# One core, attention and two MLP layers: another order of VectorE and ScalarE work at four seams, and 384 + 384 column blocks

## The chip, the core and the metric

The kernel runs on one core of a Trainium2 chip. The metric is the time of one execution on the device in microseconds (us), median of the runs shown; lower is better. Five engines work side by side, each through its own queue in order: TensorE (PE in the rows; PEld is its weight load), VectorE (DVE), ScalarE (ACT), GpSimd (POOL) and SyncE (SP, which here only issues DMAs). PE writes its results to PSUM, eight banks of 512 fp32 columns; DVE and ACT read them there. A semaphore wait at the head of a queue holds everything behind it.

## What is computed

Attention in clusters, then two MLP layers, all in fp32. The tokens of both batches are one axis of 1536.

```python
# attention: B=2, H=8, S=768, D=64; a query sees the keys of its own cluster
scores = where(q_cluster == k_cluster, q @ k.T / sqrt(D), -1e9)
attn = softmax(scores) @ v
x = attn.transpose(0, 2, 1, 3).reshape(B * S, H * D)          # 1536 x 512
# first layer: d_ff 2048
h = x @ w_in
x = (maximum(h, 0) + log1p(exp(-abs(h)))) @ w_out             # 1536 x 512
# second layer: d_ff 1536
g = x @ w_gate
out = (g / (1 + exp(-g)) * (x @ w_val)) @ w_out2
```

Weights come as fp64 and are narrowed on the chip. Each fp32 product is made of three matmuls on rounded halves: high by high, high by low, low by high.

## The kernel before

**Attention.** 16 heads go in pairs, in 96 steps of one 128-row tile each. `step(i)` issues for several tiles at once: the scores of tile i (`sc`, matmul L509, DVE row maximum L517), the exponential of tile i-1 (`ex`, ACT L525), the transposes of tile i-2 (`tr`, L541; ACT copies the high half `th` L547, DVE subtracts for the low half `tl` L548) and a third of the product with V (`pv`, L558). After the last pair `rec` makes the reciprocals `r` of the row sums on DVE, `rec_rows` transposes them on PE (L603), copies them (`R<-mps`, L606) and sends them through DRAM and back; `fin` multiplies with them and writes `XH` and `XL`, the halves of the first layer's input.

**Weights.** `w_narrow` and `w_split` take a block in three tasks: `first` (ACT absolute value, L123), `second` (two DVE passes, L125 and L128) and `third` (two DVE passes L132 and L135, then the high half `whi` L149 and the low half `wlo` L150, and the next load is issued on SP). There are three buffers for raw blocks, `raw`, and two for `m`. Tasks wait in the list `todo`; `pump` and `pump2` take some of them at set places in the code, and that alone sets the order in which they stand on DVE and ACT.

**First layer.** `h_unit(f)` makes one of 16 tiles of 128 hidden columns: 36 matmuls of 512 columns (L818) into three banks, then ACT and DVE empty the banks (`e`, `r`), two ACT passes (exponential, logarithm), a DVE sum (L888), and the halves `gh` (ACT, L858) and `gl` (DVE, L859). `y_group(g)` multiplies two such tiles with their rows of `w_out`: four groups of 18 matmuls (L908), each into three banks, which DVE adds to `acc` (L922). Units and groups alternate: two units, one group, eight times. The eight banks go round in the order in which they are asked for, so a tile's third bank can be one that an earlier tile's reader still holds. In the last group ACT also casts `acc` to `YH` (L924), and the differences `YL` go to DVE (five) or POOL (seven; L930).

**Second layer.** Of its 12 tiles, two (`plain_unit`) are plain: gate and val products of 36 matmuls each (L818), ACT Silu on the gate (L1072), a DVE product (L1081), halves (`a_half`, L973 and L974). The other ten (`s_unit`) use products of quarters; these need sums of the quarters of `acc` (`t_sums`, L1032 to L1035, four DVE subtractions of 1536 columns), and their halves `Th` (ACT, L1041) and `Tl` (DVE, L1045). Each of the ten makes seven products (`prod`, L1124): 12 matmuls that alternate 512 and 256 columns. The copy of the first (L1156) must empty its banks before the third. `o_piece` (L1096) multiplies with `w_out2` between them.

Of the kernel before, what the change touches and what calls it, by code (L numbers as in the profile page):

```python
# [11 lines left out]
F32 = mybir.dt.float32  # L12
# [28 lines left out]
def kernel(  # L41
# [18 lines left out]
    nc = tc.nc  # L60
# [130 lines left out]
    for f in range(NF2):  # L191
        stream += (pair_of(f + 1) if NPLAIN <= f + 1 < NF2 else []) + last_of(NF1 + f)
    W = {}
    loaded_t = {}
    n_load = [0]
# [9 lines left out]
    def split_tasks(batch):  # L205
# [25 lines left out]
            begun.add(tasks[-1])  # L231
        return tasks


    todo = collections.deque()

# [549 lines left out]
    for i in range(N_IT + 1):  # L786
# [8 lines left out]
        if i == 26:  # L795
            pump(2)
    rec(NP - 1)
    rec_rows(NP - 1)
    sctx.close()

# [60 lines left out]


    acc = mp.tile([128, KD, NTOK], F32, tag="acc", name="acc")
    g_t = {}

    def h_unit(f, banks=None):
        if banks is None:
            banks = [bank() for _ in range(NCH)]
            w = need(W, ("in", f))
            for half in range(2):  # L870
                proj(XH, XL, w, banks, range(2 * half, 2 * half + 2))
                pump()
# [20 lines left out]
        return [log_part, sum_part, split_part], split_tasks(batches.pop(0))  # L893

    def y_group(g):
        last = g == NF1 // 2 - 1
# [2 lines left out]
        for d0 in range(0, KD, nd):  # L899
# [15 lines left out]
            for n, bk in enumerate(banks):  # L915
# [15 lines left out]
            if not last:  # L931
                pump()

    soft0, split0 = h_unit(0, h0)
    soft1, split1 = h_unit(1, h1)
    todo.extend(split0 + [soft0[0], soft1[0], soft0[1], soft1[1], soft0[2], soft1[2]] + split1)
    pump(8)
    for g in range(NF1 // 2):
        if 2 * g + 2 < NF1:
            for f in (2 * g + 2, 2 * g + 3):  # L940
                soft, split = h_unit(f)
                if f < NF1 - 2:
                    todo.extend([soft[0]] + split[:3] + [soft[1]] + split[3:6] + [soft[2]] + split[6:])
                else:
                    first_do(soft + split[:3])
                    todo.extend(split[3:])
# [6 lines left out]
    HT = NTOK // 2  # L953
    CH = (slice(0, 512), slice(512, HT))
    outv = out.rearrange("(b p t) d -> b p t d", b=B, t=NT)
    a_t = {}
    high_on.append(1)

    def pieces_of(f):

        if f == NF2 - 1:
# [16 lines left out]
        for _ in range(-(-len(todo) // steps)):  # L978
            todo.popleft()()

    S_t, T_t = {}, {}

    def pair_tasks(f):

# [43 lines left out]

    def t_sums():

        q = [[acc[:, 2 * k:2 * k + 2, HT * t:HT * t + HT] for t in range(2)] for k in range(2)]
        nc.vector.tensor_tensor(out=q[0][0], in0=q[0][1], in1=q[0][0], op=ALU.subtract)  # L1032
        nc.vector.tensor_tensor(out=q[0][1], in0=q[1][1], in1=q[0][1], op=ALU.subtract)
        nc.vector.tensor_tensor(out=q[1][1], in0=q[1][1], in1=q[0][0], op=ALU.subtract)
        nc.vector.tensor_tensor(out=q[1][0], in0=q[1][0], in1=q[1][1], op=ALU.subtract)  # L1035
# [11 lines left out]
        tasks = []  # L1047
        for n, x in ((3, q[0][1]), (2, q[1][1]), (4, q[1][0]), (1, q[0][0])):
            tasks += [functools.partial(high, n, x), functools.partial(low, n, x)]
        return tasks  # L1050

    def plain_unit(f):
        gb = [bank() for _ in range(NCH)]
        wg = need(W, ("gate", f))
        if f == 0:
            vb = [bank() for _ in range(NCH)]
            wv = need(W, ("val", f))
            proj(YH, YL, wg, gb, range(KD - 1))
            pump2(4)
            proj(YH, YL, wv, vb, range(KD - 1))  # L1060
            pump2(3)
            proj(YH, YL, wg, gb, range(KD - 1, KD))
            proj(YH, YL, wv, vb, range(KD - 1, KD))
            pump2(2)
        else:
            for half in range(2):
                proj(YH, YL, wg, gb, range(2 * half, 2 * half + 2))
                pump2(4 - half)
        sg = tp.tile([128, NTOK], F32, tag="e", name="sg")
        for c in range(NCH):  # L1070
            cs = slice(512 * c, 512 * c + 512)
            nc.scalar.activation(out=sg[:, cs], in_=gb[c], func=AF.Silu)  # L1072
        if f:
            vb = [bank() for _ in range(NCH)]
            wv = need(W, ("val", f))
            for half in range(2):
                proj(YH, YL, wv, vb, range(2 * half, 2 * half + 2))
                pump2(2 - half)
        for c in range(NCH):
            cs = slice(512 * c, 512 * c + 512)  # L1080
            nc.vector.tensor_tensor(out=sg[:, cs], in0=vb[c], in1=sg[:, cs], op=ALU.mult)  # L1081

        def home():
            a_t[f] = pieces_of(f)

        return [home] + [functools.partial(a_half, f, sg, n) for n in range(2)]

    def o_piece(g, n, tag="O"):
        bk = psx.tile([128, 2, 512], F32, tag=tag, name="ob")
        for ff in range(2):  # L1090
            hi, lo = need(W, ("out2", 2 * g + ff))
            ah, al = (x[n // 3] for x in a_t[2 * g + ff])
            for t in range(2):
# [21 lines left out]
    def s_unit(f):  # L1115
# [3 lines left out]
        def prod(dst, group, at, x, first=False):  # L1119
            hi, lo = group  # L1120
            for kk in range(2):
                for wt, part in ((hi, 0), (hi, 1), (lo, 0)):
                    for cs in CH:
                        nc.tensor.matmul(  # L1124
                            dst[:, cs],
                            lhsT=wt[:, at + kk, :],
                            rhs=x(part, kk)[:, cs],
                            start=(first and kk == 0 and wt is hi and part == 0),
                            stop=(kk == 1 and wt is lo),
                            skip_group_check=True,  # L1130
# [17 lines left out]
            pump2(left[0])  # L1148
            left[0] -= 1

        t1, t2 = slice(0, HT), slice(HT, NTOK)
        sg = tp.tile([128, NTOK], F32, tag="e", name="sg")
        x = psx.tile([128, 1024], F32, tag="X", name="x")[:, 0:HT]
        prod(x, g1, 0, quarter(0, 0), True)
        p1 = p1_p.tile([128, HT], F32, tag="p1", name="p1")
        nc.scalar.copy(p1, x)  # L1156
        more()
        w = psx.tile([128, 1024], F32, tag="W", name="w")[:, 0:HT]
        prod(w, g2, 0, tq(3), True)
        nc.scalar.copy(sg[:, t2], w)  # L1160
        more()
# [13 lines left out]
        y = psx.tile([128, 1024], F32, tag="Y", name="y")[:, 0:HT]  # L1175
# [11 lines left out]
        a_half(f, sg, 0)  # L1187
        a_half(f, sg, 1)

    side = [tp.tile([128, NTOK], F32, tag="s", name="side") for _ in range(2)]  # L1190
    todo.extend(t_sums())
    todo.extend(split_tasks(last_of(NF1)))
    todo.extend(plain_unit(0))
    todo.extend(pair_tasks(2))
    todo.extend(split_tasks(last_of(NF1 + 1)))
    rest = plain_unit(1)
    while todo:
        todo.popleft()()
# [63 lines left out]
```

## Time and profile before

| | us |
|---|---|
| median of 3 runs | 815.05 |
| runs | 814.87 to 816.88 |
| profiled execution | 813.9 |
| its span, first to last instruction | 812.1 |
| PE busy in the span | 791.0 |
| DVE busy | 654.5 |
| ACT busy | 500.8 |
| POOL busy | 163.0 |

The profiled execution is 1.15 us under the median; 1.8 us of it lie outside the span. The mean granted PE clock is 0.994 of full speed. A matmul's record is longer than its step, since matmuls overlap in the pipeline; so the pace of PE is read from the starts of neighbours.

### The profile page before, as it was taken

What the parts mean: (1) busy time and instruction counts of PE and PEld (TensorE: products, weight loads), DVE (VectorE), ACT (ScalarE), POOL (GpSimd) and SP (SyncE); (2) the same over time, 40 slices, a digit from 0 to 9 for tenths busy, and PEclk for the clock granted to TensorE, in tenths of its full rate; (3) what the DMA queues carried; (4) which work ended last, traced back from release to release, by engine and by line L of the source; (5) the groups of instructions that cost most, each with busy time, mean ns of one, the idle gap of its engine ahead of it and who ended that gap; (6) DMA issues with size and microseconds to landing.
All of it is one profiled execution on the core that took longest, in us unless ns stands there. A gap on an engine that the chain in (4) does not pass through costs nothing.

```text
span 812.1 us, 12093 instructions
## 1 busy us (share of the span) xinstructions
PE 791.0 (97%) x4485; PEld 689.6 (85%) x4485; DVE 654.5 (81%) x1047; ACT 500.8 (62%) x893; POOL 163.0 (20%) x160
## 2 busy tenths in 40 slices
PE   8999999999999999999999999989999999999997
PEld 7898999999998778888888887867888888888886
DVE  6988988888895997989879778889777777777763
ACT  5888889889895587365563744355544655555520
POOL 5736456555522000000000000400000101011100
PEclk9999999999999999999999999999999999999999
DMA  7875865675411322222121210012435676767454
GB/s 177 238 180 128 204 145 145 168 164 138 98 40 31 104 78 78 76 81 78 52 78 55 76 52 28 25 39 92 155 132 115 144 147 138 154 120 142 85 176 155
DMA packets 69339, 91.57 MB, mean 113 GB/s; under 512 B 29376, under 2 KB 52000, under 8 KB 69280
## 3 DMA queue, kind: packets, MB, share of 16 engines
q1 hardware_dynamic: 64688, 79.40, 34.6%
q0 software_dynamic: 3024, 11.01, 9.0%
q8 instruction: 35, 0.57, 0.3%
q10 hardware_dynamic: 1568, 0.39, 0.2%
q14 instruction: 24, 0.20, 0.1%
HBM read 51.41 MB, written 17.35 MB: 85 GB/s over the span
## 4 chain that ended last, share of the span: by engine, by line
PE 81%; DVE 12%; ACT 3%; DMA 2%; issue 1%; POOL 0%; DVEq 0%; ACTq 0%; SPq 0%; POOLq 0%
PE bank L908 14%; PE bank L818 13%; PE ob L1096 12%; PE x L1124 10%; PE ops L558 7%; PE tps L541 7%; PE sps L509 7%; PE w L1124 5%; PE y L1124 3%; PE mps L383 1%; PE sims L420 1%; DVE m L135 1%; DVE m L132 1%; DVE acc L922 1%; DVE wlo L150 1%
## 5 line engine op out<-in xcount | busy, mean ns | idle before, releaser
L548 DVE TENSOR_TENSOR tl<-tps,th 128x384 fp32r<-128x384 f32 x192 | 98.8, 550 | 14.8 <-ACT th L547 14.5
L517 DVE TENSOR_REDUCE nm<-sps 128x1 f32<-128x768 f32 x96 | 91.3, 952 | 14.1 <-PE sps L509 11.5
L547 ACT CAST th<-tps 128x384 fp32r<-128x384 f32 x192 | 84.6, 490 | 18.6 <-PE tps L541 16.0
L541 PE MATMUL tps<-id,p 128*128 128x128 f32 x576 | 93.1, 278 | 1.5 <-DVE tl L548 1.5
L525 ACT ACTIVATE p<-sps,nm 128x768 f32<-128x768 f32 x96 | 88.2, 919 | 1.6 <-DVE nm L517 1.6
L509 PE MATMUL sps<-KT,QT 128*128 128x384 f32 x384 | 83.4, 339 | 1.7 <-ACT p L525 1.7
L541 PEld LDWEIGHTS tps<-id,p 128*128 128x128 f32 x576 | 75.1, 151 | 8.1 <-DVE tl L548 4.2
L558 PE MATMUL ops<-th,VV 128*128 128x256 f32 x288 | 80.1, 307 | 0.0
L558 PE MATMUL ops<-tl,VV 128*128 128x256 f32 x288 | 72.7, 282 | 0.0
L858 ACT CAST gh<-e 128x1536 fp32r<-128x1536 f32 x16 | 23.8, 1487 | 73.0 <-DVE e L888 73.0
L509 PEld LDWEIGHTS sps<-KT,QT 128*128 128x128 f32 x384 | 63.3, 189 | 2.6 <-ACT p L525 2.4
L1113 POOL DMA_DIRECT2D out_dram<-side x21 | 18.2, 868 | 227.5 <-ACT side L1109 227.5
L150 DVE TENSOR_TENSOR wlo<-m,whi 128x512 fp32r<-128x512 f32 (+1 forms) x66 | 43.0, 651 | 24.2 <-ACT whi L149 22.5
L930 POOL TENSOR_TENSOR YL<-acc,YH 128x512 fp32r<-128x512 f32 x7 | 9.3, 1322 | 260.6 <-ACT YH L924 260.4
L922 DVE TENSOR_TENSOR acc<-bank,acc 128x512 f32<-128x512 f32 x84 | 53.0, 681 | 6.4 <-PE bank L908 6.4
L908 PE MATMUL bank<-gh,whi 128*128 128x512 f32 x192 | 54.5, 391 | 2.2 <-DVE whi L149 1.1
L1096 PE MATMUL ob<-whi,aa 128*128 128x512 f32 x168 | 56.5, 390 | 0.0
L558 PEld LDWEIGHTS ops<-tl,VV 128*128 128x128 f32 x288 | 54.7, 190 | 0.1
L818 PE MATMUL bank<-XH,whi 128*128 128x512 f32 x192 | 54.1, 390 | 0.7 <-DVE whi L149 0.7
L558 PEld LDWEIGHTS ops<-th,VV 128*128 128x128 f32 x288 | 54.4, 189 | 0.2
L908 PE MATMUL bank<-gl,whi 128*128 128x512 f32 x192 | 54.0, 389 | 0.0
L908 PE MATMUL bank<-gh,wlo 128*128 128x512 f32 x192 | 54.0, 389 | 0.0
(199 smaller groups left out, 1938.4 us busy)
## 6 DMA issues: line engine op xcount, KB each, us to landing
raw<-in_moe_w_out_dram SPq DMA_DIRECT2D x28, 512.0 KB, 3.3
out_dram<-side POOLq DMA_DIRECT2D x21, 512.0 KB, 5.6
raw<-in_moe_w_in_dram SPq DMA_DIRECT2D x16, 512.0 KB, 3.7
raw<-in_moe_w_val_dram SPq DMA_DIRECT2D x12, 512.0 KB, 4.4
raw<-in_moe_w_gate_dram SPq DMA_DIRECT2D x12, 512.0 KB, 3.4
QT<-hi SPq DMA_DIRECT2D x30, 192.0 KB, 3.0
KT<-hi SPq DMA_DIRECT2D x14, 384.0 KB, 5.6
kn<-in_k_dram SPq DMA_DIRECT2D x16, 192.0 KB, 3.9
```

Source lines behind the costliest of these rows:

```text
L509: nc.tensor.matmul(ps[:, c, 0:384], lhsT=Q[:, a, 128 * j:128 * j + 128], rhs=K[:, a, 384 * c:384 * c + 384], start=(a == 0), stop=(a == 1),)
L517: nc.vector.tensor_reduce(out=nm, in_=ps[:, :, 0:384], axis=AX.XY, op=ALU.max, negate=True)
L525: nc.scalar.activation(out=_h(p), in_=s_t.pop(i)[:, :, 0:384], func=AF.Exp, bias=nm_t.pop(i), accum_out=sm_t[pr][:, j:j + 1],)
L541: nc.tensor.transpose(ps[:, 128 * j:128 * j + 128], p[:, 128 * kb:128 * kb + 128], id32)
L547: nc.scalar.copy(th, pv)
L548: nc.vector.tensor_tensor(out=tl, in0=pv, in1=_r(th), op=ALU.subtract)
L558: nc.tensor.matmul(o[:, 0:CW], lhsT=VV_t[pr][:, hh, kb].rearrange("p a d -> p (a d)"), rhs=t[:, kb, :], start=(kb == 0 and lohi == 0), sto ...
L818: nc.tensor.matmul(banks[c], lhsT=wt[:, kk, :], rhs=xt[:, kk, 512 * c:512 * c + 512], start=(kk == 0 and wt is hi and xt is xh), stop=(kk ...
L908: nc.tensor.matmul(banks[NCH * d + c], lhsT=wt[:, 0, ds_], rhs=gt[:, 512 * c:512 * c + 512], start=(ff == 0 and n == 0), stop=(ff == 1 and ...
L922: nc.vector.tensor_tensor(out=a, in0=bk, in1=a, op=ALU.add)
L1096: nc.tensor.matmul(bk[:, t, :], lhsT=lhs[:, ts_], rhs=rhs[:, 0, :], start=(ff == 0 and i == 0), stop=(ff == 1 and i == 2),)
L1124: nc.tensor.matmul(dst[:, cs], lhsT=wt[:, at + kk, :], rhs=x(part, kk)[:, cs], start=(first and kk == 0 and wt is hi and part == 0), stop= ...
```

## The change

Seven edits.

1. `step(N_IT + 1)`, the last transposes and a part of `pv`, is called between `rec` and `rec_rows`, not after them.
2. The two `w_out` blocks 0 and 1 are put on the list before the first tile's matmuls, and two `pump(1)` stand between these.
3. The block `in 3` is worked off as a whole before the first tile's ACT and DVE work.
4. In the last pair of units the list is emptied in a written order: `out 14` and `out 15` first, `gate 1` (of which ACT's part comes early) in the last but one group.
5. In the last group, `out2 0` and `out2 1` go together (`two_tasks`), a piece after each of its four parts, with the first quarter difference (`t_sum(0)`) after the third. The other three follow as one task with three `Th` casts; the fourth cast and `Tl` move behind the Silu of unit 0. A Silu of one column is put ahead, so that the table of that function is loaded there.
6. The products of the ten tiles are 384 + 384 columns in two banks, where they were 512 + 256.
7. In the very last `o_piece` the two banks are filled one after the other.

```diff
     rec(NP - 1)
+    step(N_IT + 1)
     rec_rows(NP - 1)
...
+    todo.extend(split_tasks(batches.pop(0)))
     for n in range(3):
-        step(N_IT + 1 + n)
+        if n:
+            step(N_IT + 1 + n)
         proj(XH, XL, w0, h0, range(n, n + 1))
+        if n < 2:
+            pump(1)
...
-    todo.extend(split_tasks(batches.pop(0)))
-    pump(4)
+    pump(2)
...
+    run(split_tasks(batches.pop(0)))
+    batches.insert(0, [])
     soft0, split0 = h_unit(0, h0)
...
+        if 2 * g + 4 == NF1:
+            split = split_tasks([w for _ in range(2) for w in batches.pop(0)])
+            out0, gate, out1 = (split[3 * n:3 * n + 3] for n in range(3))
+            soft = h_unit(NF1 - 2, None, [[*todo], [out0[0]]])
+            todo.clear()
+            run([out1[0], soft[0], *out0[1:], soft[1], *out1[1:], gate[0], soft[2]])
+            soft = h_unit(NF1 - 1, None, [[], []])
+            run(soft[:1])
+            after = [soft[1:2], soft[2:3], gate[1:], []]
...
+            high_on.append(1)
+            out0 = two_tasks([("out2", f) for f in range(NPLAIN)], "b")
+            run(out0[:1])
+            after = [out0[1:2], out0[2:3], [functools.partial(t_sum, 0)], out0[3:]]
...
+        if f == 0:
+            nc.scalar.activation(out=side[0][:, 0:1], in_=id32[:, 0:1], func=AF.Silu)
...
-                    for cs in CH:
+                    for c in range(2):
                         nc.tensor.matmul(
-                            dst[:, cs],
+                            dst[:, c, :],
                             lhsT=wt[:, at + kk, :],
-                            rhs=x(part, kk)[:, cs],
+                            rhs=x(part, kk)[:, HT // 2 * c:HT // 2 * c + HT // 2],
```

How instructions stand in the queues, at three places.

PE at the end of attention, before: the transposed reciprocals (`mps<-id_72,r`) stand ahead of the last six transposes.

```order
L558 MATMUL ops<-tl,VV 128x256
L603 MATMUL mps<-id_72,r 12x128
L541 MATMUL tps<-id_72,p 128x128 x6
L558 MATMUL ops<-th,VV 128x256
L558 MATMUL ops<-tl,VV 128x256
```

The same place after the change:

```order
L568 MATMUL tps<-id_72,p 128x128 x6
L585 MATMUL ops<-th,VV 128x256
L585 MATMUL ops<-tl,VV 128x256
L585 MATMUL ops<-th,VV 128x256
L585 MATMUL ops<-tl,VV 128x256
L585 MATMUL ops<-th,VV 128x256
L585 MATMUL ops<-tl,VV 128x256
L630 MATMUL mps<-id_72,r 12x128
L846 MATMUL bank<-XH,whi 128x512 x3
```

The reciprocals moved behind six transposes and six products.

DVE from the second part of the last `y_group` on, before: bank additions and `YL`, then the four quarter differences (`acc<-acc`), then `gate 1`.

```order
L930 TENSOR_TENSOR YL<-acc,YH 128x512
L922 TENSOR_TENSOR acc<-bank,acc 128x512 x3
L930 TENSOR_TENSOR YL<-acc,YH 128x512
L922 TENSOR_TENSOR acc<-bank,acc 128x512 x3
L930 TENSOR_TENSOR YL<-acc,YH 128x512
L922 TENSOR_TENSOR acc<-bank,acc 128x512
L930 TENSOR_TENSOR YL<-acc,YH 128x512
L1032 TENSOR_TENSOR acc<-acc 128x2x768
```

DVE there after the change, from the second `YL` on:

```order
L982 TENSOR_TENSOR YL<-acc,YH 128x512
L974 TENSOR_TENSOR acc<-bank,acc 128x512
L132 SCALAR_TENSOR_TENSOR m<-raw,m 128x512
L135 SCALAR_TENSOR_TENSOR m<-raw,m 128x512
L132 SCALAR_TENSOR_TENSOR m<-raw,m 128x512
L135 SCALAR_TENSOR_TENSOR m<-raw,m 128x512
L974 TENSOR_TENSOR acc<-bank,acc 128x512 x2
L982 TENSOR_TENSOR YL<-acc,YH 128x512
L974 TENSOR_TENSOR acc<-bank,acc 128x512
L940 TENSOR_TENSOR acc<-acc 128x2x768
```

Passes of `out2` (eight in all, four of them in the part before this piece) and one difference now stand between the bank additions.

ACT at the start of the second layer, before: four `Th` casts, the table load, the Silu of unit 0.

```order
L1041 CAST Th<-acc 128x1536 x4
L1072 ACT_TABLE_LOAD
L1072 ACTIVATE sg<-bank 128x512 x3
L123 ACTIVATE m<-raw 128x512
L149 CAST whi<-m 128x512
```

ACT there after the change:

```order
L149 CAST whi<-m 128x512 x2
L1096 CAST Th<-acc 128x1536 x3
L1131 ACT_TABLE_LOAD
L1131 ACTIVATE side<-id_72 128x1
L1134 ACTIVATE sg<-bank 128x512 x3
L1096 CAST Th<-acc 128x1536
```

One cast moved behind the Silu; the table load has the one-column Silu behind it.

## Rows read from the trace of the kernel before

**Rows 1.** Waits of PE: who waited for whom, us in total, times, longest.

```profile
PE bank L908 <- ACT r L881: 1.1, 1, 1.1
```

**Rows 2.** The chain that ended last: start us, us, engine, tile, line, matmuls.

```profile
223.79 0.96 PE sps L509 x4
...
243.14 0.70 PE sps L509 x4
...
307.72 16.32 PE bank L818 x72
...
583.64 2.11 PE x L1124 x12
```

**Rows 3.** Timeline, end of attention: start, us, engine, line, operation [idle before <-releaser].

```profile
251.44 1.02 DVE L548 TENSOR_TENSOR tl<-tps,th 128x384 fp32r<-128x384 f32 x2 [0.68 <-ACT th L547]
251.51 0.28 PE L558 MATMUL ops<-tl,VV 128*128 128x256 f32 x1
...
252.86 0.28 PE L603 MATMUL mps<-id,r 128*12 128x128 f32 x1 [1.06 <-DVE r L597]
...
254.35 0.86 PE L818 MATMUL bank<-XH,whi 128*128 128x512 f32 x3
```

**Rows 4.** Timeline, first units and the first group of layer 1.

```profile
264.28 0.43 DVE L125 TENSOR_SCALAR m<-m 128x512 f32<-128x512 f32 x1
...
281.24 0.96 PE L818 MATMUL bank<-XH,whi 128*128 128x512 f32 x3 [0.74 <-DVE whi L149]
...
289.37 1.88 DVE L879 TENSOR_SCALAR r<-bank 128x512 f32<-128x512 f32 x3
```

**Rows 5.** Timeline, the last two groups of layer 1.

```profile
487.08 0.84 PE L908 MATMUL bank<-gh,whi 128*128 128x512 f32 x3
...
506.72 0.94 PE L908 MATMUL bank<-gh,whi 128*128 128x512 f32 x3 [1.12 <-DVE whi L149]
...
521.13 0.84 PE L818 MATMUL bank<-YH,whi 128*128 128x512 f32 x3
```

**Rows 6.** Timeline, unit 0 and the start of unit 1 of layer 2.

```profile
524.84 1.75 DVE L1032 TENSOR_TENSOR acc<-acc 128x1536 f32<-128x1536 f32 x1
...
534.00 5.60 ACT L1041 CAST Th<-acc 128x1536 fp32r<-128x1536 f32 x4
...
539.62 1.28 ACT L1072 ACT_TABLE_LOAD   x1
...
541.56 0.50 PE L818 MATMUL bank<-YH,whi 128*128 128x512 f32 x1 [3.50 <-ACT sg L1072]
```

**Rows 7.** Windows: PE, PEld, DVE, ACT, POOL busy, PEclk, DMA share, GB/s.

```profile
541.50:546.30 4.80, 4.74 (x14) 3.74 (x15) 4.70 (x8) 1.55 (x4) 0.00 (x0) 0.64 0.00 0
```

**Rows 8.** Timeline, first tile of the ten.

```profile
559.17 0.50 PE L1124 MATMUL x<-YH,whi 128*128 128x512 f32 x2
...
564.60 0.62 PE L1124 MATMUL x<-Th,whi 128*128 128x512 f32 x2 [1.03 <-ACT p L1156]
```

**Rows 9.** Groups by line, DVE: busy us, mean ns of one.

```profile
L922 DVE TENSOR_TENSOR acc<-bank,acc 128x512 f32<-128x512 f32 x84 | 53.0, 681 | 6.4 <-PE bank L908 6.4
L135 DVE SCALAR_TENSOR_TENSOR m<-raw,m 128x512 int32<-128x512 int32 x68 | 47.1, 692 | 2.3
...
L125 DVE TENSOR_SCALAR m<-m 128x512 f32<-128x512 f32 x68 | 28.6, 421 | 16.6 <-ACT m L123 16.6
```

**Rows 10.** Timeline, start of the kernel: POOL and DVE on SBUF data.

```profile
9.97 1.83 POOL L680 TENSOR_TENSOR khl<-xr,khl 128x768 fp32r<-128x768 f32 x1 [0.25 <-ACT khl L678]
...
10.98 1.05 DVE L650 TENSOR_TENSOR eq<-eq,wi 128x192 f32<-128x192 f32 x1
...
13.61 0.36 DVE L650 TENSOR_TENSOR eq<-eq,wi 128x192 f32<-128x192 f32 x1
```

**Rows 11.** Tile YL: count, duration ns min/median/max, first and last start.

```profile
L930 POOL TENSOR_TENSOR YL<-acc,YH x7: 1291/1299/1472, 511.8 to 522.9; 128x512 fp32r<-128x512 f32 x7
L930 DVE TENSOR_TENSOR YL<-acc,YH x5: 692/692/956, 511.2 to 524.2; 128x512 fp32r<-128x512 f32 x5
```

More of the change, by code (lines that the diff above doesn't have):

```diff
@@ L190 @@
     stream = [w for batch in batches for w in batch]
-    for f in range(NF2):
-        stream += (pair_of(f + 1) if NPLAIN <= f + 1 < NF2 else []) + last_of(NF1 + f)
+    stream += [w for f in range(NPLAIN) for w in last_of(NF1 + f)] + pair_of(NPLAIN)
+    for f in range(NPLAIN, NF2):
+        stream += (pair_of(f + 1) if f + 1 < NF2 else []) + last_of(NF1 + f)
     W = {}
@@ L232, in split_tasks, with two_tasks, first, second @@
         return tasks
+    def two_tasks(keys, tag):
+        m_t = {}
+        def first():
+            for key in keys:
+                while key not in loaded_t:
+                    load_ahead(len(loaded_t) + 1)
+                m_t[key] = w_narrow(loaded_t.pop(key))
+                next(m_t[key])
+        def second():
+            for key in keys:
+                next(m_t[key])
+        def third():
+            for key in keys:
+                m_t[key] = next(m_t[key])
+            load_ahead(3)
+        def split(key):
+            pool, bufs = pool_of[tag]
+            W[key] = w_split(m_t[key], pool, tag, bufs)
+        return [first, second, third] + [functools.partial(split, key) for key in keys]
     todo = collections.deque()
@@ L863, with run, h_unit @@
     acc = mp.tile([128, KD, NTOK], F32, tag="acc", name="acc")
+    after = []
     g_t = {}
-    def h_unit(f, banks=None):
+    def run(tasks):
+        for task in tasks:
+            task()
+    def h_unit(f, banks=None, between=None):
         if banks is None:
@@ L871, in h_unit @@
                 proj(XH, XL, w, banks, range(2 * half, 2 * half + 2))
-                pump()
+                if between is None:
+                    pump()
+                else:
+                    run(between[half])
         e = tp.tile([128, NTOK], F32, tag="e", name="e")
@@ L891, in split_part, with t_sum @@
             g_t[f] = split_g(e, "g")
-        return [log_part, sum_part, split_part], split_tasks(batches.pop(0))
+        soft = [log_part, sum_part, split_part]
+        return soft if between else (soft, split_tasks(batches.pop(0)))
+    HT = NTOK // 2
+    quad = [[acc[:, 2 * k:2 * k + 2, HT * t:HT * t + HT] for t in range(2)] for k in range(2)]
+    T_t = {}
+    def t_sum(n):
+        nc.vector.tensor_tensor(
+            out=quad[(0, 0, 1, 1)[n]][(0, 1, 1, 0)[n]],
+            in0=quad[(0, 1, 1, 1)[n]][(1, 1, 1, 0)[n]],
+            in1=quad[(0, 0, 0, 1)[n]][(0, 1, 0, 1)[n]],
+            op=ALU.subtract,
+        )
     def y_group(g):
@@ L930, in y_group @@
                     low.popleft()()
-            if not last:
+            if after:
+                run(after.pop(0))
+            elif not last:
                 pump()
+    run(split_tasks(batches.pop(0)))
+    batches.insert(0, [])
     soft0, split0 = h_unit(0, h0)
@@ L979, in pump2 @@
             todo.popleft()()
-    S_t, T_t = {}, {}
+    S_t = {}
     def pair_tasks(f):
@@ L1029, in t_sums @@
     def t_sums():
[L1031 to L1035, printed above, removed]
         def high(n, x):
@@ L1045, in low, with sums @@
             nc.vector.tensor_tensor(out=_h(tl), in0=x, in1=_r(_h(th)), op=ALU.subtract)
[L1047 to L1050, printed above, removed]
+        def sums():
+            for n in range(1, 4):
+                t_sum(n)
+            for n, x in order[:3]:
+                high(n, x)
+        order = ((3, quad[0][1]), (2, quad[1][1]), (4, quad[1][0]), (1, quad[0][0]))
+        return [sums] + [functools.partial(low, n, x) for n, x in order[:3]] + [
+            functools.partial(high, *order[3]), functools.partial(low, *order[3])
+        ]
     def plain_unit(f):
@@ L1057, in plain_unit @@
             wv = need(W, ("val", f))
+            for _ in range(4):
+                todo.popleft()()
             proj(YH, YL, wg, gb, range(KD - 1))
-            pump2(4)
             proj(YH, YL, wv, vb, range(KD - 1))
-            pump2(3)
             proj(YH, YL, wg, gb, range(KD - 1, KD))
             proj(YH, YL, wv, vb, range(KD - 1, KD))
-            pump2(2)
         else:
@@ L1089, in o_piece @@
         bk = psx.tile([128, 2, 512], F32, tag=tag, name="ob")
[L1090 to L1093, printed above, removed]
+        turns = [(t, ff) for ff in range(2) for t in range(2)]
+        if (g, n) == (NF2 // 2 - 1, 5):
+            turns.sort()
+        for t, ff in turns:
+                hi, lo = need(W, ("out2", 2 * g + ff))
+                ah, al = (x[n // 3] for x in a_t[2 * g + ff])
                 ts_ = slice(256 * (n % 3) + 128 * t, 256 * (n % 3) + 128 * t + 128)
@@ L1174, in s_unit @@
         more()
-        y = psx.tile([128, 1024], F32, tag="Y", name="y")[:, 0:HT]
+        y = psx.tile([128, 2, 512], F32, tag="Y", name="y")[:, :, 0:HT // 2]
         prod(y, g1, 2, quarter(1, 0), True)
@@ L1186, in s_unit @@
         fill(2)
-        a_half(f, sg, 0)
-        a_half(f, sg, 1)
+        a_half(f, sg_all, 0)
+        a_half(f, sg_all, 1)
     side = [tp.tile([128, NTOK], F32, tag="s", name="side") for _ in range(2)]
     todo.extend(t_sums())
[L1192 to L1195, printed above, removed]
+    rest = plain_unit(0)
+    todo.extend(rest)
+    todo.extend(pair_tasks(NPLAIN))
     rest = plain_unit(1)
```

22 lines of the change are left out of this document (8 added, 14 removed).

## The prediction

> **What bounds the kernel now.** I read the waits of PE first, then the chain that ended last, then the timeline around each wait. PE is the bound almost everywhere. The chain shows the pace of undisturbed stretches: 72 matmuls of 512 columns in 16.32 us, 0.2267 us each [rows 2]. From the third product of the first of the ten tiles on (564.60) PE never waits again. So the reader should look for places where PE falls behind this pace, and they all lie between 251 and 565 us, at the four seams that the change touches. I measure each loss as the distance between two starts less the matmuls between them at that pace.
>
> **The losses of before.**
> Attention's end: PE has its last product at 251.51 and is free some 0.12 later, then waits for the reciprocals until 252.86; the first layer starts at 254.35 [rows 3].
> Layer 1's start: from 254.35 to 281.24 PE has 108 matmuls and 12 small ones (1.42 us by their own steps), 25.9 us, and takes 26.9: 1.0 lost, to the high half of a `w_in` block [rows 3, 4]. From 281.24 to 307.72, 108 matmuls are 24.48 us and take 26.48: 2.0 lost, mostly to an ACT pass that empties a bank [rows 1, 2, 4].
> Layer 1's end: from 487.08 to 521.13, 144 matmuls are 32.64 us and take 34.05: 1.4 lost, to the high half of `out 15` [rows 5].
> Unit 0 and 1: from 521.13 to 559.17, 144 matmuls are 32.64 us and take 38.04: 5.4 lost. 3.5 is the wait for the Silu that frees the third bank of unit 1 [rows 6, 8]; after it the granted clock is 0.64 on average over 4.8 us, part of it at the lower level of 1.2 GHz, which makes up the rest [rows 7]. Before the fall PE had stood idle for 3.5 us.
> First of the ten tiles: two products of 2.11 from 559.17 end at 563.39, the third starts at 564.60: 1.2 lost, 1.3 with a slow restart [rows 2, 8].
>
> **Part by part.**
> *Edit 1.* The six transposes can start when DVE has emptied their banks: its two `tl` run from 251.44 to 252.46 [rows 3]. So PE starts at about 252.05 and 252.53, ends its six products near 253.65, turns the reciprocals and begins the first layer at 253.7, where it was 254.35: 0.6 gained. The copy of `R` now queues on DVE behind two `tl` and an addition, some 1.7 us later, and with it two DMAs on SP; their reader feeds the fourth slice of XH, which PE reads only after 27 more matmuls of the second tile (6.1 us). That is the cover, and I cost it at nothing.
> *Edits 2 and 3.* One weight block is worked off while DVE waited before, and `in 3` comes before the six bank passes, about 9 us before its use. The loss of 1.0 goes. What is late next: the third bank of the first group, which DVE empties with `r` at 289.37 [rows 4]. Ahead of it DVE had four weight blocks and two passes, of 0.42 each, of a fifth; now it has four blocks alone, 0.85 less, and starts on them 0.3 earlier. So `r` comes at 288.2, and PE can go on at 288.9. PE itself arrives 1.6 us earlier, at 288.3. That leaves a wait of 0.6. The ACT wait behind it goes, because the block that its `m` buffer waited for is done 5 us sooner. Of 2.0 I count 1.4.
> *Edit 4.* `out 15` is done before the last group begins. By the queue `gl` of the last tile ends four us before it is read, `gate 1` ends before the last bank additions. 1.4 gained. SP issues the load of `out2 1` when `gate 1` leaves its buffer, early enough for ACT, which would hold the `YH` casts behind it.
> *Edit 5.* This is the large one. With edit 4 the last group starts at 503.40 (487.08 + 16.32), its four parts end every 4.08, unit 0 starts at 519.72, and PE wants the bank that the first Silu frees 74 matmuls later, at 536.5 [rows 2, 5]. DVE has in the last group 12 additions of 0.68, five `YL` of 0.69, and newly four passes of 0.42, four of 0.69 and a difference of 1.75, 17.8 us [rows 6, 9, 11]. From the first bank at 507.2 that is 525.0 if nothing stands in the way; two `wlo` of 0.69 and three differences, 1.86 apart, bring 532.0. Then the third cast (1.4), the table load (1.28) and about 0.8 for the small and the first Silu: PE could go on at 535.6 [rows 6]. So without any interference the Silu wait vanishes with 0.9 to spare, and the slow clock with it: 5.4 gained.
> But POOL makes seven `YL` in the same stretch. The rows show that DVE and POOL hold each other up on SBUF data: the product of `eq` takes 1.05 beside a POOL subtraction that ends at 11.80, and 0.36 alone [rows 10]; a DVE `YL` that met POOL took 956 ns where 692 is the median, and POOL's slowest 1472 where 1299 is [rows 11]. The bank additions, with one side in PSUM, show no such thing (mean 681) [rows 9]. In the order of before DVE had nearly only these between; now it has passes on SBUF there. If the two take turns, each of the first three parts costs DVE about 0.6 for POOL's first `YL` (the rest lies beside an addition) and 1.2 for the second: 5.4. About 1.3 of it falls where DVE would wait anyhow. DVE is then 4.1 later, the Silu wait ends at about 539.9 by the same steps with their joints, and PE loses 3.4 in all (1.2 of it already at unit 0's third bank, whose addition slips past 520.2), 3.7 with restarts. No stretch of it is as long as the idle time that came before the slow clock, so I leave the clock high. Bounds: 0 with no interference, 7.5 if the Silu comes as late as before and the clock falls too.
> On such meetings the Trainium skill has a rule (SBUF — State Buffer, section SBUF: two separate sides): DVE and GpSimd share one port pair, whoever starts first holds it for the whole instruction and the other is blocked. By that rule the term is the 3.7, without it 0; the rows agree as far as they go.
> For the table load the row gives 1.28, and the Silu follows at once [rows 6]. The Trainium skill (ScalarE: Activation LUTs, What ACT_TABLE_LOAD costs) adds a drain of 1.38 to each switch. This trace shows none; by the page the Silu would be 1.4 later and the sum 1.4 higher.
> *Unit 0 to the first of the ten.* The two `out2` blocks no longer stand between unit 1's last matmul and its products on DVE. ACT gets to the copy that the third product waits for before PE does, by some 0.4. 1.3 gained.
> *Edit 6.* There are 840 matmuls in 70 products. Four of 384 columns take 0.70 in attention, so twelve take 2.10, where 512 + 256 take 2.11: 0.7 over 70 products [rows 2]. Rounding of the rows leaves -1.5 to 2.8; I take 0.7.
> *Edit 7.* DVE's two additions of a piece already start after the whole piece, and one semaphore count still stands at its end: 0.
>
> **Sum.** 0.6 + 1.0 + 1.4 + 1.4 + 5.4 + 1.3 + 0.7 = 11.8, less 3.7, is 8.1. The profiled span goes from 812.1 to 804.0, its execution from 813.9 to 805.8, and the median, which lies 1.15 above, from 815.05 to about 807.0.
>
> **The rivals.**
> *No interference that matters:* DVE's passes slip in between POOL's and all seams close. For it: POOL's delays cost little in the rows of before. 803.3.
> *The Silu as late as before:* DVE loses every turn, PE stands over 3 us in one piece, and the clock falls again. 7.5 of new loss in place of 3.7: 810.8. Against it: one difference fewer and one cast fewer stand ahead of the Silu. The table switch with a drain lies between, at 808.4.
> *The seams stay shut:* freed time at the start of layer 1 or in unit 0 is given back to a load or a bank that comes late next; little is left, 813 to 817. The order of the queues speaks against it.
> *Slower:* the blocks of 384. If one costs more than the mean of 512 and 256, 0.176, it is paid 840 times. Four of them took 0.96 where PE had to start them from a stand [rows 2], 0.24 each, which would be 54 us more, 861; the whole gain is gone from 0.1855 on, and at 0.19 the time is 820. Against it: nearly all other groups of four take 0.70 or 0.71, 0.175 each.
>
> **How the numbers follow.** My forecast, with its own range of 805 to 809, has 0.47; no interference 0.25; the late Silu with its variant 0.18; seams that stay shut 0.06; slower 0.04. The prediction is the likeliest, 807.0. The range takes in the first three and the rounding of edit 6: 802.5 to 811.5. About 0.3%, 2.4 us, can be told from no change: faster 0.90, same 0.06, slower 0.04.
>
> **What would show it.** After the change PE should have no wait on `whi` at the third unit or in the last group, none on the copy `p` of the first product, and the first layer should start about 0.6 earlier. In the last group POOL's `YL` and DVE's passes should show lengthened records; DVE's last difference should end about 16.6 us after unit 0's start if they take turns, about 12.3 if not. A granted clock under 1 near unit 1 would be the late Silu. Groups of twelve in the ten tiles should take 2.10. If PE waits at places that no row here names, the sum is wrong.

## The result and the profile after

| | before | after |
|---|---|---|
| median, us | 814.96 | 806.23 |
| runs, us | 813.12 to 816.88 | 804.0 to 807.81 |
| ratio to before, 95% interval | | 0.9891 (0.9858 to 0.9923) |
| profiled execution, us | 813.9 | 804.0 |
| its span, us | 812.1 | 802.2 |
| granted PE clock, mean | 0.994 | 0.997 |

The changed kernel is faster by 8.7 us, 1.1%; 807.0 was predicted, 802.5 to 811.5 the range. Measured twice more, beside the experiments, it gave 0.9878 (0.9864 to 0.9892) and 0.9885 (0.9864 to 0.9907).

Where the time went is read from start to start of the same matmuls in both traces. The letters are used below. A stop is the distance between two neighbouring starts less the step that the pace allows; a wait is the idle time that the profile shows there, and is some 0.1 to 0.2 shorter.

| stretch of PE | before | after | gained | forecast |
|---|---|---|---|---|
| start to the last scores | 247.63 | 247.02 | 0.61 | 0 |
| A: last scores to first layer | 6.72 | 6.01 | 0.71 | 0.6 |
| B: first layer to its fourth tile | 26.89 | 26.07 | 0.82 | 1.0 |
| C: fourth tile to fifth tile | 26.32 | 25.12 | 1.20 | 1.4 |
| D: fifth tile to seventh group | 179.52 | 179.52 | 0 | 0 |
| E: seventh group to unit 0 | 34.05 | 32.64 | 1.41 | 1.4 |
| F: unit 0 to the first of the ten tiles | 38.05 | 35.13 | 2.92 | 5.4 - 3.7 |
| G: its first two products | 5.42 | 4.19 | 1.23 | 1.3 |
| H: third product to the last | 215.59 | 214.60 | 0.99 | 0.7 |
| I: the rest | 31.94 | 31.93 | 0 | 0 |

The first line is chance. Over the fourteen profiles of this study the last scores started anywhere from 246.99 to 250.48, and the thirteen kernels of after and of the experiments are the same code up to there. So a median can't tell 1 us from nothing here, and most stretches can: D is 179.52 in every profile. B and C are less sure: in the ten profiles with the order of the changed kernel there, they take 51.19 to 51.86 together, so that 1.3 to 2.0 is gained and the profile of the result is the best case.

The starts that no other rows show, of before:

```profile
307.56 0.84 PE L818 MATMUL bank<-XH,whi 128*128 128x512 f32 x3
```

Of the changed kernel:

```profile
279.10 0.84 PE L846 MATMUL bank<-XH,whi 128*128 128x512 f32 x3
...
304.22 0.84 PE L846 MATMUL bank<-XH,whi 128*128 128x512 f32 x3
...
483.74 0.84 PE L960 MATMUL bank<-gh,whi 128*128 128x512 f32 x3
...
516.38 0.61 PE L846 MATMUL bank<-YH,whi 128*128 128x512 f32 x2
...
551.51 0.51 PE L1188 MATMUL x<-YH,whi 128*128 128x384 f32 x2
...
555.70 0.51 PE L1188 MATMUL x<-Th,whi 128*128 128x384 f32 x2
```

The waits of PE in the changed kernel, from 252 us on (who waited for whom, total, times, longest):

```profile
PE bank L846 <- ACT sg L1134: 1.0, 1, 1.0
PE bank L960 <- DVE r L918: 0.3, 1, 0.3
PE bank L846 <- POOL YL L982: 0.3, 1, 0.3
PE bank L846 <- DVE acc L974: 0.3, 1, 0.3
```

Four waits are left of six, with one of 0.27 just ahead of 252 (shown below). The waits on `whi`, on the reciprocals and on the copy `p` are gone; the Silu wait of [rows 6] is 1.0 where it was 3.5. The timeline of PE where attention ends, and of DVE and PE in the first group:

```profile
251.44 1.01 PE L568 MATMUL tps<-id,p 128*128 128x128 f32 x6 [0.27 <-DVE tl L575]
...
253.00 0.27 PE L630 MATMUL mps<-id,r 128*12 128x128 f32 x1
253.03 0.94 PE L846 MATMUL bank<-XH,whi 128*128 128x512 f32 x3
...
287.48 1.88 DVE L918 TENSOR_SCALAR r<-bank 128x512 f32<-128x512 f32 x3
...
288.21 0.50 PE L960 MATMUL bank<-gh,whi 128*128 128x512 f32 x1 [0.34 <-DVE r L918]
```

The transposes wait 0.27 for `tl` (DVE's low half) where the reciprocals waited 1.06 [rows 3]. `r` comes 34.45 after the first layer's start, where [rows 4] have 35.02.

DVE and POOL in the last group and at the start of unit 0 (the second POOL row of 518.44 stands alone in the last line):

```profile
505.88 0.68 DVE L974 TENSOR_TENSOR acc<-bank,acc 128x512 f32<-128x512 f32 x1
505.91 2.73 POOL L982 TENSOR_TENSOR YL<-acc,YH 128x512 fp32r<-128x512 f32 x2 [252.12 <-ACT YH L976]
506.48 1.01 DVE L125 TENSOR_SCALAR m<-m 128x512 f32<-128x512 f32 x1
...
507.52 1.40 DVE L128 TENSOR_SCALAR m<-m 128x512 int32<-128x512 int32 x1
...
512.21 1.27 DVE L132 SCALAR_TENSOR_TENSOR m<-raw,m 128x512 int32<-128x512 int32 x1
...
513.52 1.66 DVE L135 SCALAR_TENSOR_TENSOR m<-raw,m 128x512 int32<-128x512 int32 x1
...
519.01 2.35 DVE L940 TENSOR_TENSOR acc<-acc 128x1536 f32<-128x1536 f32 x1
```

```profile
519.82 2.69 POOL L982 TENSOR_TENSOR YL<-acc,YH 128x512 fp32r<-128x512 f32 x1
```

Read the ends: POOL's first `YL` runs from 505.91 to 507.20, and DVE's pass of 0.42, begun at 506.48, ends 0.29 after that. The difference begun at 519.01 ends at 521.36, and the `YL` that POOL began at 519.82 ends 1.15 later, where it takes 1.30 alone. Both ends come 0.13 to 0.15 sooner than a whole length behind the other engine's end; no run shows why. Five DVE records are longer by 0.59, 0.97, 0.58, 0.97 and 0.60, 3.7 in all. The bank addition at 505.88, with one input in PSUM, takes its 0.68 beside POOL, and POOL's `YL` its 1.29.

ACT and PE at unit 1's third bank, and the window behind it (its columns are those of [rows 7]):

```profile
531.93 1.49 ACT L1096 CAST Th<-acc 128x1536 fp32r<-128x1536 f32 x1 [0.31 <-DVE acc L940]
...
533.43 1.28 ACT L1131 ACT_TABLE_LOAD   x1
...
534.73 0.20 ACT L1131 ACTIVATE side<-id 128x1 f32<-128x1 f32 x1
534.84 1.55 ACT L1134 ACTIVATE sg<-bank 128x512 f32<-128x512 f32 x3
535.47 0.50 PE L846 MATMUL bank<-YH,whi 128*128 128x512 f32 x1 [1.04 <-ACT sg L1134]
```

```profile
535.00:540.00 5.00, 4.53 (x20) 3.72 (x21) 5.00 (x6) 2.76 (x4) 0.00 (x0) 1.00 0.00 0
```

The granted clock is 1.00 there, the upper level (2.4 GHz). The chain in the ten tiles shows the products of 384 columns, where [rows 2] have 2.11:

```profile
553.78 2.08 PE w L1188 x12
...
638.49 2.10 PE x L1188 x12
```

### The profile page after: what moved, and what is told of

Read it like the earlier page. It is cut to its first block, busy times and chain, and to the rows that moved or that the text cites. A ratio compares the mean times of both kernels' runs of the same rounds, so it can differ in the third digit from the quotient of the medians.

```text
span 802.2 us, 12088 instructions
## 1 busy us (share of the span) xinstructions
PE 787.8 (98%) x4485; PEld 705.1 (88%) x4485; DVE 659.1 (82%) x1048; ACT 501.2 (62%) x893; POOL 164.5 (21%) x160
## 4 chain that ended last, share of the span: by engine, by line
PE 86%; DVE 8%; ACT 3%; DMA 2%; issue 1%; POOL 0%; DVEq 0%; ACTq 0%; SPq 0%; POOLq 0%
PE bank L846 15%; PE bank L960 15%; PE ob L1160 12%; PE x L1188 10%; PE ops L585 8%; PE tps L568 7%; PE sps L536 7%; PE w L1188 5%; PE y L1188 3%; PE mps L410 2%; PE sims L447 1%; DVE acc L940 1%; DVE m L135 1%; DVE m L132 1%; DMA R<-rd 1%
## 5 line engine op out<-in xcount | busy, mean ns | idle before, releaser
L846 PE MATMUL bank<-XL,whi 128*128 128x512 f32 x192 | 53.9, 389 | 0.0
```

The source lines that it names most:

```text
L846: nc.tensor.matmul(banks[c], lhsT=wt[:, kk, :], rhs=xt[:, kk, 512 * c:512 * c + 512], start=(kk == 0 and wt is hi and xt is xh), stop=(kk ...
```

## The experiments

Theory: the changed order closes the seams, and what is left of the Silu wait comes from DVE and POOL taking turns. The rivals are named with each run. One table holds all of them; the stretches are those above (B and C together), in us. The kernels were measured in three sets, and each ratio is to the runs of before in the same set. The four kernels with an edit undone have no run of the changed kernel in their set, so they are compared by the stretches. Edits 2, 4 and 7 were not undone alone.

| kernel | median | ratio (95%) | A | B+C | E | F | G | H |
|---|---|---|---|---|---|---|---|---|
| before (three sets) | 814.95 to 815.09 | 1 | 6.72 | 53.21 | 34.05 | 38.05 | 5.42 | 215.59 |
| after, again | 805.72 | 0.9878 (0.9864 to 0.9892) | 6.00 | 51.78 | 32.64 | 35.11 | 4.19 | 214.60 |
| after, third time | 806.18 | 0.9885 (0.9864 to 0.9907) | 6.01 | 51.33 | 32.64 | 35.13 | 4.19 | 214.60 |
| edit 5 undone | 807.54 | 0.9918 (0.9894 to 0.9941) | 6.01 | 51.42 | 32.64 | 32.64 | 7.36 | 216.13 |
| POOL idle | 802.64 | 0.9842 (0.9827 to 0.9856) | 6.00 | 51.26 | 32.64 | 32.64 | 4.19 | 214.60 |
| all `YL` on DVE | 805.32 | 0.9883 (0.9863 to 0.9903) | 6.01 | 51.19 | 32.64 | 34.37 | 4.19 | 214.60 |
| no one-column Silu | 806.36 | 0.9888 (0.9867 to 0.9909) | 6.01 | 51.70 | 32.64 | 35.02 | 4.19 | 214.60 |
| table early | 804.87 | 0.9868 (0.9854 to 0.9882) | 6.00 | 51.20 | 32.64 | 33.75 | 4.48 | 214.63 |
| table early, `out2` late | 803.82 | 0.9868 (0.9848 to 0.9889) | 6.01 | 51.48 | 32.64 | 32.91 | 4.49 | 214.65 |
| the same, two more moves | 801.56 | 0.9833 (0.9816 to 0.9850) | 6.01 | 50.90 | 32.64 | 32.81 | 4.18 | 214.60 |
| edit 1 undone | 805.58 | 0.9895 (0.9880 to 0.9910) | 6.73 | 51.11 | 32.64 | 35.11 | 4.19 | 214.60 |
| edit 3 undone | 808.85 | 0.9930 (0.9907 to 0.9952) | 6.02 | 52.79 | 32.64 | 35.11 | 4.19 | 214.60 |
| edit 6 undone | 807.13 | 0.9915 (0.9891 to 0.9939) | 6.01 | 51.86 | 32.64 | 35.15 | 4.23 | 215.48 |

The changed kernel stands in it twice, as the mark that the others of its set are compared with:

> The changed kernel again, as the mark for the others of this set. 0.989 of the kernel before (0.987 to 0.992), with three stops of PE between the last y_group and unit 1: about 0.4 at the third bank of unit 0, 0.4 at its YL, 1.2 at the third bank of unit 1. If these stops are chance and not built into the order, they come at other places or with other lengths.

> The changed kernel once more, as the mark for this set: 0.988 of the kernel before (0.986 to 0.990).

The three stops between the last group and unit 1 came back at the same matmuls with the same lengths, within 0.03 us. They belong to the order.

**Is it POOL?**

```diff
-    low.append(functools.partial(eng.tensor_tensor, out=YL[:, d, cs], in0=a, in1=_r(YH)[:, d, cs], op=ALU.subtract))
+    if eng is nc.gpsimd:
+        low.append(functools.partial(nc.scalar.copy, YL[:, d, cs], a))
+    else:
+        low.append(functools.partial(eng.tensor_tensor, out=YL[:, d, cs], in0=a, in1=_r(YH)[:, d, cs], op=ALU.subtract))
```

> The seven YL of POOL in the last y_group are replaced by plain copies on ACT, so that part of the low halves is left out and POOL does nothing there; DVE's queue is unchanged. Theory (DVE and POOL take turns): the four passes of 0.42 in the first part, the two of 0.69 in the second and the first difference take 0.41 to 0.43, 0.69 and 1.75 again where they took 1.01, 1.40, 1.27, 1.66 and 2.35; DVE's last difference ends 3.7 earlier, at about 12 us after unit 0's start where it was 15.5; the three stops of 2.07 in all are gone, and the time is about 2.0 under the changed kernel. Rival (the passes are long for another reason, as their own operands or ACT's work): the same lengths, the last difference still at 15 to 16, the stops stay, no gain.

This kernel leaves out seven of the low halves, and ACT has seven copies more. The same passes of DVE in that kernel's timeline:

```profile
506.52 0.42 DVE L125 TENSOR_SCALAR m<-m 128x512 f32<-128x512 f32 x1
506.97 0.43 DVE L128 TENSOR_SCALAR m<-m 128x512 int32<-128x512 int32 x1
...
510.70 0.68 DVE L132 SCALAR_TENSOR_TENSOR m<-raw,m 128x512 int32<-128x512 int32 x1
...
515.93 1.75 DVE L940 TENSOR_TENSOR acc<-acc 128x1536 f32<-128x1536 f32 x1
...
523.21 5.33 DVE L940 TENSOR_TENSOR acc<-acc 128x1536 f32<-128x1536 f32 x3
```

All have their short times (`m` of L135 too, 0.69), the last difference ends at 528.54, 12.1 after unit 0's start (15.5 in the changed kernel), and from 500 to 560 us PE waits for nothing. F falls to 32.64, which is 144 matmuls at full pace. So the turn-taking costs 2.49 in F, 2.07 of it in the three stops and the rest in the slower steps behind them. The rival is out.

**The other remedy: no POOL, and its work on DVE.**

```diff
-    eng = nc.gpsimd if c == 1 or c == 2 and d < KD - 1 else nc.vector
+    eng = nc.vector
```

> All twelve YL of the last y_group on DVE, none on POOL. By DVE's work alone this adds 7 x 0.69 = 4.8, and the stop at unit 1's third bank would grow from 1.2 to about 6. If DVE and POOL take turns, 3.7 of stretched passes goes at the same time: DVE's last difference ends only about 1.1 later, at 16.6 after unit 0's start, and that stop is about 2.3, with no wait for POOL's YL: about 1 over the changed kernel.

The expectation missed to the good side. The timeline of DVE:

```profile
510.21 0.68 DVE L974 TENSOR_TENSOR acc<-bank,acc 128x512 f32<-128x512 f32 x1
510.81 0.68 DVE L982 TENSOR_TENSOR YL<-acc,YH 128x512 fp32r<-128x512 f32 x1
511.41 0.68 DVE L974 TENSOR_TENSOR acc<-bank,acc 128x512 f32<-128x512 f32 x1
...
527.31 5.34 DVE L940 TENSOR_TENSOR acc<-acc 128x1536 f32<-128x1536 f32 x3
```

In a queue that is full, additions and `YL` start 0.60 apart, though each has a record of 0.68. Seven more passes cost 4.2, not 4.8. Against that, the 3.7 of longer records go, and so does 0.9 of DVE's idle time, which the expectation did not count: the largest piece was a wait of 0.69 for ACT's last `YH`. The last difference ends 14.7 after unit 0's start, 0.7 earlier than with POOL's help. The two stops of 0.4 go, the wait for the Silu is 1.36: F is 0.75 shorter. By this stretch POOL's help costs more than it gives; the medians don't show it. The granted clock behind that wait:

```profile
536.30:541.30 5.00, 5.00 (x22) 4.15 (x23) 4.82 (x5) 2.43 (x4) 0.00 (x0) 1.00 0.00 0
```

**Which edit closed the Silu wait?** Edit 5 undone: `out2`, differences, casts and Silu in the order of before (a part of it):

```diff
-            out0 = two_tasks([("out2", f) for f in range(NPLAIN)], "b")
-            run(out0[:1])
-            after = [out0[1:2], out0[2:3], [functools.partial(t_sum, 0)], out0[3:]]
...
+    todo.extend(split_tasks(last_of(NF1)))
+    todo.extend(plain_unit(0))
+    todo.extend(pair_tasks(2))
+    todo.extend(split_tasks(last_of(NF1 + 1)))
```

> Edit 5 is undone in the changed kernel: out2, the four differences, the four casts and the Silu stand in the order of before; edit 4 and the others stay. If edit 5 is what closed the Silu wait, PE stops for about 3.5 at the third bank of unit 1, the granted clock falls behind it, unit 0 to the ten tiles takes 38.0 where the changed kernel takes 35.1, and the first of the ten loses 1.2 again: about 4.1 over the changed kernel. If the earlier out 15 and gate 1 of edit 4 had closed it, DVE is ahead by itself and the stretch stays under 36.

The first theory fell: without edit 5 F takes 32.64, and of the edits left only edit 4 lies in this part of the kernel. The reason stands on ACT's queue. Before, from its timeline, a row ahead of the four casts of [rows 6]:

```profile
533.47 0.62 ACT L149 CAST whi<-m 128x512 fp32r<-128x512 f32 x1 [9.27 <-DVE m L135]
```

With edit 5 undone:

```profile
525.01 1.49 ACT L1098 CAST Th<-acc 128x1536 fp32r<-128x1536 f32 x1 [4.34 <-DVE acc L1090]
...
533.42 1.58 ACT L1129 ACTIVATE sg<-bank 128x512 f32<-128x512 f32 x3
```

Before, the casts stood behind the high half of a block, which waited for two DVE passes, which stood behind all four differences. Edit 4 puts this block, `gate 1`, into the last but one group; the first cast comes 7.4 after unit 0's start where it came 12.9, and the Silu is in time. But the wait comes back two seams on, with the second `out2` block (ACT, PE and the window behind the stop):

```profile
552.69 0.62 ACT L149 CAST whi<-m 128x512 fp32r<-128x512 f32 x1 [2.61 <-DVE m L135]
555.27 1.56 ACT L1030 CAST YH<-sg 128x768 fp32r<-128x768 f32 x2 [1.96 <-DVE sg L1138]
556.74 0.79 ACT L1216 COPY p<-x 128x768 f32<-128x768 f32 x1
```

```profile
557.59 1.01 PE L1183 MATMUL x<-Th,whi 128*128 128x384 f32 x2 [3.00 <-ACT p L1216]
```

```profile
557.60:561.00 3.40, 3.40 (x11) 3.40 (x12) 3.12 (x7) 1.76 (x3) 0.00 (x0) 0.54 0.02 5
```

PE stands for 3.00 before the third product, and the granted clock behind it is 0.54 on average over 3.4 us, most of it at the lower level (1.2 GHz). So edit 4 gains 1.41 in E, as far as the order of the queues tells, and 5.41 in F, and 3.47 of this is given back in G and H (7.36 and 216.13 against 5.42 and 214.60). Edit 5 takes these, 1.53 of them slow clock, and the 1.23 that G had lost before: 4.70 for 2.49 of turn-taking, 2.21 net.

**What the one-column Silu does.**

```diff
-        if f == 0:
-            nc.scalar.activation(out=side[0][:, 0:1], in_=id32[:, 0:1], func=AF.Silu)
```

> The one-column Silu is left out. Where the change has it, it stands right ahead of the Silu that needs the table, behind the casts. If it hides nothing there, the table load comes at the same time, the stop at unit 1's third bank is 0.1 shorter (1.1), and the time is the same within 0.3. If it hides the load, the stop grows by up to 1.3.

F is 0.1 shorter without it, the stop 1.13 instead of 1.21. Where it stands it hides nothing. Put ahead of the casts, it falls into ACT's idle time (the added line; the old place goes):

```diff
+            nc.scalar.activation(out=side[0][:, 0:1], in_=id32[:, 0:1], func=AF.Silu)
             for n, x in order[:3]:
                 high(n, x)
```

> The one-column Silu stands ahead of the three Th casts, not behind them, so the table load falls into ACT's idle time before the casts. If the 1.2 at unit 1's third bank is the load behind the casts on ACT's queue, the first Silu ends some 1.3 earlier, that stop goes and the two of 0.4 stay: about 1.2 less than the changed kernel. If the table is lost again to the casts, a second load shows ahead of the Silu and nothing is gained.

```profile
527.61 1.28 ACT L1105 ACT_TABLE_LOAD   x1
...
535.29 1.56 ACT L1133 ACTIVATE sg<-bank 128x512 f32<-128x512 f32 x3
```

The casts leave the table in place, and the Silu stop is gone. F gains 1.36 and G loses 0.29: PE now comes to the first of the ten tiles before the halves of its first blocks are ready. The list of PE's waits does not show this, but its weight load (PEld) waits there:

```profile
552.07 0.30 PEld L1187 LDWEIGHTS x<-YH,whi 128*128 128x128 f32 x2 [0.25 <-ACT whi L149]
...
552.98 0.30 PEld L1187 LDWEIGHTS x<-YH,wlo 128*128 128x128 f32 x2 [0.26 <-DVE wlo L150]
```

In the changed kernel PEld has no wait there.

**A better order.** First, on top of the early table, `out2`'s larger passes and the first difference behind the last additions:

```diff
-            after = [out0[1:2], out0[2:3], [functools.partial(t_sum, 0)], out0[3:]]
+            after = [out0[1:2], [], [], [out0[2], functools.partial(t_sum, 0)] + out0[3:]]
```

> As the kernel with the early table load, and besides out2's passes of 0.69 and the first difference stand behind the last bank additions. If the two stops of 0.4 are DVE passes (in part those stretched beside POOL) that stand ahead of bank additions and YL, they go as well: about 2.0 under the changed kernel. If the loads that these passes set off are now too late, PE waits for a gate or val block of the first ten-loop tiles, after 545 us, and the gain is under 1.

The two stops of 0.4 go; F and G together take 37.40, where the changed kernel takes 39.3. At full pace they would take 36.82: 0.58 is lost to late halves, for which the weight load waits 0.42 and 0.26. Then two more moves:

```diff
-            if f < 3:
+            if f < 2 or f == 2 and c:
...
+    todo.extend(pair_tasks(NPLAIN))
     todo.extend(rest)
-    todo.extend(pair_tasks(NPLAIN))
```

> As the kernel with the early table load and the late out2 passes, with two more moves: the first r pass of the third tile goes to ACT, and the narrowing of the first blocks of the ten tiles stands ahead of unit 0's halves. Theory: the wait for r in the first group (0.5 to 0.8) goes, since ACT empties that bank some 3 us before PE asks for it, and the 0.6 of slow starts in the first of the ten, which lie at blocks that are narrowed late, go too: fourth to fifth unit 24.6 where it is 25.1 to 25.4, unit 0 to the third product of the ten 36.8 to 36.9 where the changed kernel takes 39.3; in all some 3 under the changed kernel. Rival: the next bank comes late in their place, and less than 2.3 is gained.

ACT empties the bank of `r` at 283.7, and the table is loaded at 523.3:

```profile
283.72 0.60 ACT L920 ACTIVATE r<-bank 128x512 f32<-128x512 f32 x1
...
523.25 1.28 ACT L1105 ACT_TABLE_LOAD   x1
```

From 252 us on PE's matmuls wait for nothing that the trace names. Its weight load still waits 0.25 for the Silu at unit 1's third bank (532.83), and 0.17 is lost in F. C is 24.48, F and G 36.99, and the median 801.56, 0.9833 (0.9816 to 0.9850) of before beside 0.9885 (0.9864 to 0.9907) for the changed kernel on the same chip. This version beats both. Of the 4.6 between the two medians the stretches explain 2.8: 0.43 in B and C, 2.33 in F and G.

**The other edits, one at a time.** Edit 1 undone:

```diff
     rec(NP - 1)
-    step(N_IT + 1)
     rec_rows(NP - 1)
...
-        if n:
-            step(N_IT + 1 + n)
+        step(N_IT + 1 + n)
```

> Edit 1 is undone: the reciprocals' transposes stand ahead of the last six transposes again. From the last scores to the first layer it should take 6.7 where the changed kernel takes 6.0. If PE is the bound behind it, the whole is 0.7 longer. Rival: the wait for r in the first group (0.5 to 0.8 in the changed kernel) is set by DVE, which does not start later; then that wait takes up the loss, and the start of the fifth unit is only 0 to 0.3 later.

```profile
252.49 0.27 PE L630 MATMUL mps<-id,r 128*12 128x128 f32 x1 [1.08 <-DVE r L624]
...
253.99 0.86 PE L845 MATMUL bank<-XH,whi 128*128 128x512 f32 x3
```

A takes 6.73, as before, and nothing comes back in B and C (51.11 beside 51.19 to 51.86): 0.72 is its worth. The medians of the two kernels don't show it.

Edit 3 undone:

```diff
-    run(split_tasks(batches.pop(0)))
-    batches.insert(0, [])
     soft0, split0 = h_unit(0, h0)
```

> Edit 3 alone is undone: in 3 stands behind the first two tiles' ACT and DVE work again; out 0 and 1 stay early. If in 3's place is the cause of the stop at the fourth unit and of the late r behind it, the stop of 0.9 comes back (first to fourth unit 26.9 where it is 26.1) and the next stretch is 26.3 where it is 25.1 to 25.4: about 1.8 longer. If edit 2 had given DVE enough room, both stretches stay within 0.3.

```profile
282.15 0.96 PE L846 MATMUL bank<-XH,whi 128*128 128x512 f32 x3 [0.22 <-DVE whi L149]
...
296.55 0.50 PE L960 MATMUL bank<-gh,whi 128*128 128x512 f32 x1 [1.14 <-ACT r L920]
```

B and C take 52.79: edit 3 is worth 0.9 to 1.6, less than the 1.8 expected. The wait at the fourth tile comes back at 0.2, not 0.7, so edit 2 has most of that one; the wait for ACT's `r` comes back whole.

Edit 6 undone (a part of it):

```diff
-                    for c in range(2):
+                    for cs in CH:
```

> Edit 6 is undone: the products of the ten tiles are 512 + 256 columns in one row of 1024 again. If 384 + 384 is the gain in the ten tiles, the 67 products from the third of the first tile to the last take 215.6 where the changed kernel takes 214.6, and the whole is 1.0 longer. If the gain there came from another edit (fewer tasks left on DVE and ACT), the stretch stays at 214.6 and so does the time.

H takes 215.48 where it takes 214.60, so the gain there is the columns' and not that of fewer tasks left over. Edit 7 was not tried alone; I is the same with and without it.

## Why the prediction was right, and where it was not

- **Attention's end, 0.6.** 0.71, and the first layer starts as forecast behind the reciprocals. PE waits for nothing from there to the first group, so the later copy of `R` is covered.
- **Layer 1's start, 1.0 and 1.4.** 0.82 and 1.20 in the profile of the result, and 1.3 to 2.0 together over all profiles, so 0.4 to 1.1 too much was forecast. One reading was wrong: the chain's row at 307.72 begins 0.16 after the fifth tile's first matmul (307.56), so the second loss was 1.84 and not 2.0. The `r` that was to come late next did, 34.45 after the first layer's start where the working gives 34.5, with a stop of 0.5 where 0.6 was forecast; in other profiles of the same order the wait there is up to 0.7, where the result has 0.34.
- **Layer 1's end, 1.4.** 1.41, to full pace in all thirteen profiles, also with edit 5 undone. Edit 4 was not undone, so that the gain is its own rests on the order of the queues.
- **Edit 5, "this is the large one", 5.4.** The step that failed is the credit. I read the late Silu as DVE's last difference alone and did not count what stood ahead of the casts on ACT. That was `gate 1`, which edit 4 moves; edit 4 closes the wait and the clock loss by itself (what edit 5 does without edit 4 was not run). Edit 5 is needed for the seam behind it, where I counted 1.3 and where 4.7 is at stake once PE arrives earlier. The sum holds, since both edits were in it; that is luck and not insight.
- **Take turns, less 3.7.** The mechanism was right, the size was not: 2.49. DVE's records are 3.7 longer and not 5.4: 1.2 of this because in the third part it was POOL that had to wait for DVE's difference, the rest because the second meeting of the first two parts cost 0.97 each and not 1.2. The last difference ends 15.5 after unit 0's start, between the 16.6 and the 12.3 named as signs. Without POOL it ends at 12.1, so the turns delay it by 3.4, where 4.1 was forecast. I had also priced a full queue by its records, 0.68 and 0.69, where its steps are 0.60; the 12.1 beside the 12.3 shows that this made little here. The Trainium skill's rule (SBUF — State Buffer, section SBUF: two separate sides), that whoever starts first holds the shared port pair for the whole instruction, agrees with the rows in both directions; the bank additions, with one input in SBUF, keep their 0.68 and are outside it.
- **The clock stays high.** It did (1.00). PE's longest idle time there is 1.04. It fell after 3.50 before, and after 3.00 with edit 5 undone.
- **The table load, 1.28.** The next instruction starts at once, 0.01 behind it, in every profile shown here. The drain of 1.38 that the Trainium skill adds (ScalarE: Activation LUTs, section What ACT_TABLE_LOAD costs) does not appear.
- **Blocks of 384, 0.7.** 0.99, and 0.88 with the edit undone; products take 2.08 to 2.10. The rival of a dearer block is out. One figure of the working does not come out: the rounding of its rows leaves -0.7 to 2.1, not -1.5 to 2.8.

By these stretches 9.28 was gained, 8.1 forecast: 1.2 too much taken off for the turns, 0.3 too little for the blocks, and 0.4 the other way at layer 1's start. That the median came within 0.8 of the forecast is in part chance: the profiled execution is 1.8 under its own forecast (804.0 against 805.8), and the start up to the last scores alone scatters by 3.5. This scatter is not explained here.

## What to carry to other kernels

A wait that ends with an engine's instruction is priced by that engine's whole queue ahead of it: look for the one instruction there that waits for a third engine. An order that closes one seam brings the bound earlier to the next, so price each edit again with the others in place. And before work is given to POOL beside a busy DVE, count what the two lose by taking turns; here DVE alone was 0.75 faster in the stretch concerned.

## What the runs showed of the hardware

- A DVE pass on SBUF data and a POOL `YL` do not run together: 0.42 becomes 1.01 and 1.40, 1.75 becomes 2.35, and POOL's 1.30 becomes 2.69. With POOL idle all of DVE's are short. A DVE addition with one side in PSUM keeps its 0.68 beside POOL.
- DVE's additions and `YL` in a full queue, none of which needs the one ahead, start 0.60 apart where each record is 0.68 long.
- A table loaded by a one-column Silu (527.61) outlasts three casts on ACT: no second load stands ahead of the Silu at 535.29.
- PE's granted clock was 1.00 behind idle times of 1.04 (the changed kernel) and 1.36 (all `YL` on DVE). It was 0.54 on average behind 3.00 (edit 5 undone, over 3.4 us) and 0.64 behind 3.50 (before, over 4.8 us).
